# The end of a fused attention and expert kernel: last blocks with tokens on partitions, and three smaller edits

## The chip, the cores and the metric

The kernel runs on one core of a Trainium2 chip. A core has a matrix engine (TensorE, PE in the profile; its weight loads are shown apart as PEld), three engines for elementwise work (VectorE or DVE, ScalarE or ACT, GpSimd or POOL) and queues that issue transfers (SP, and ACT's and POOL's own). They run side by side, each in its own order, and wait for one another on semaphores. Matrix products go to PSUM, in banks of 512 float32 per partition; PE, DVE and ACT work on PSUM, POOL here only on SBUF. The metric is the device time of one execution in microseconds: 448.48 us, the median of three runs (448.10 to 449.16).

## The reference, cut to what matters

A polynomial attention is followed by four experts, all of which every token goes through:

```python
q_p, k_p = phi(q), phi(k)                  # 64 products of two 8-wide sketches
num = q_p @ (k_p.T @ v);  den = q_p @ k_p.sum(0) + 1e-06
x = (num / den)                            # (4, 4, 1088, 32) -> 4352 tokens x 128
p = domain_probs / (domain_probs.sum(-1, keepdims=True) + 1e-09)
for e in range(4):                         # w1: 128 x 1024, w2: 1024 x 128
    h = np.maximum(x @ w1[e], 0.0)
    out += p[:, e:e + 1] * (h @ w2[e])
```

Everything is float32.

## The kernel before

The experts take nearly all the time. Tokens are cut into ten chunks (`CHUNKS`, line 105): 128, 448, six of 480, two of 448. Activations lie transposed, with features on partitions and tokens along the columns. A step `i` of the main loop is a chunk `m`, an expert `e` and a pair of the eight 128-wide blocks of the hidden layer; its two halves, one block each, are the half-steps that plans and due times count. There are 160 steps; `work()` counts half-steps in `now` and runs whatever `lay_plan` has put down for that count: the attention of later tokens, which is spread between the expert's work by hand (`UNITS_AT`: for each unit of queries the half-steps of its transpose, of its two products, and of its use).

First layer, per block (`first`, `third`): three matmuls in a fast float32 form with operands split in a high and two low parts, `xa·wa` (L1140), `xb·wb` (L1141), ACT scales the sum in PSUM (L1142), and one half-step later `xd·wd` (L1192). A block then goes one of two ways. A three-part block: ACT writes the high part `ha` (L1196), DVE the low part `hb` (L1168) and, for two blocks at once, `hd` (L1171), and the second layer multiplies three parts. A plain block: ACT writes the relu (L1201) and the second layer multiplies it in full float32, four times the columns' time, in two records on PE.

Second layer: `to_due` puts each product on a list with its half-step by the `DEAL` tables (a letter for the part, x for plain; a number for the block), and `behind` issues what is due. Products a and b go to one PSUM bank (o0), d and x to the other (o1); `last_of` names the one that ends a bank. When o0 ends, ACT scales it to SBUF (`ev`, L1268). When o1 ends, `gather` adds it to ev, POOL multiplies by the gate row (L1337) and adds to `total` (L1339). For chunks before the seventh the addition of o1 is done by DVE (L1324); from the seventh on ACT copies o1 (L1327) and POOL adds (L1330). `ev` has one buffer.

The last chunk's last expert (`at_end`) has six three-part blocks (0, 1, 3, 4, 5, 6) and then two plain ones (2, 7), and an ending of its own: POOL gates and adds o0's share in two halves (L1272, L1273), while the last matmul is cut in two halves; then per half DVE multiplies o1 by the gate (L1288), adds the total (L1289), transposes 32x32 squares (L1290), and four stores write runs of 32 floats (L1293), on SP's and ACT's queues.

The query units: a unit's projection goes to memory (`qd`) and comes back with rows repeated in `qp` and `qb` (L779, L781); `unit_product` multiplies the two on DVE (L793). Each chunk's tokens are split in parts four and three steps before its first (L893 on ACT, L896 on DVE). The key projection (L458) multiplies 128-wide weights by 128 columns in plain float32.

Of the kernel before, what the change touches and what calls it, by code (L numbers as in the profile page):

```python
# [7 lines left out]

F32 = mybir.dt.float32
BF16 = mybir.dt.bfloat16  # L10
# [2 lines left out]
ALU = mybir.AluOpType  # L13
# [11 lines left out]
def kernel(  # L25
# [24 lines left out]
    nc = tc.nc  # L50

    P = 128
# [33 lines left out]
        b5=9, a6=9, a7=9, b6=10, b7=10, d4=10, d5=11, d6=11, d7=12,  # L86
    )
    DEAL_END = dict(
        a0=4, b0=4, a1=4, b1=5, a2=5, a3=5, d0=6, d1=6, b2=6, a4=7, b3=7, a5=8, b4=8, d2=8, d3=8,
        b5=9, d4=10, d5=10, x6=10, x7=11,  # L90
    )
    ALL_IN = {(7, 2), (8, 2), (9, 2)}
    UNITS = [[P, 448, 512], [576, 512], [576, 512], [576, 512]]
# [7 lines left out]
    W2_AT = (36, 37, 38, 39, 40), (40, 41, 42, 43, 44), (45, 46, 48, 50, 53), (51, 53, 56, 60, 63)  # L101
    TOKENS_AT = 11, 12

    CHUNKS = [P, 448] + [480] * 6 + [448] * 2
    NC = len(CHUNKS)
    MORE_IN = {(2, 2), (3, 2), (4, 2), (5, 0), (5, 2), (5, 3), (6, 2), (7, 0), (7, 1), (7, 2), (7, 3), (8, 0), (8, 1), (8, 2), (8, 3), (9, 0), (9, 1), (9, 2)}
    MORE_AT = {0: (73, 75), 1: (56, 57), 2: (38, 39), 3: (77, 78)}
# [85 lines left out]

    def last_of(m, e, o):
        deal = deal_of(m, e)
        return max((p for p in deal if (p[0] in "ab") == (o == 0)), key=lambda p: (deal[p], list(deal).index(p)))

    def split_at(b):
        return (THREE if in_three(b) else OTHER).index(b)
# [175 lines left out]
    def parts(m):  # L375

        c, end, at = START[m], START[m] + CHUNKS[m], 0
        while c < end:
            n = min(end, (c // S + 1) * S) - c
            yield c // S, c % S, n, at  # L380
            c, at = c + n, at + n
# [420 lines left out]
    def add(hs, run):  # L802
# [9 lines left out]

    UNITS_AT = (
        (30, 43, 44, 47), (41, 71, 77, 79), (68, 103, 106, 111), (102, 134, 137, 143), (132, 161, 171, 175),
        (172, 180, 196, 207), (200, 217, 219, 223),
    )

    def lay_plan():
# [253 lines left out]
    def at_end(m, e):  # L1072
        return (m, e) == (NC - 1, E - 1)
# [85 lines left out]
    def hidden():  # L1159
        return mpool.tile([P, CW], F32, tag="hid", bufs=4, name="hid")  # L1160
# [26 lines left out]
    def third():  # L1187

        while begun:
            i, j, k, g, w, x = begun.pop(0)  # L1190
            n = g.shape[-1]
            nc.tensor.matmul(g, w, x, start=False, stop=True, skip_group_check=True)  # L1192
            m, e = steps[i][0], steps[i][1] // NP
            if k in three_of(m, e) and not whole(m, e):
                (ha, hb, hc), both_of = three_tiles(k, n, three_of(m, e))
                nc.scalar.activation(ha, g, ACTF.Relu, scale=NEAR)  # L1196
                to_lower.append((g, ha.bitcast(F32), hb, both_of))
                hid[i][j] = ha, hb, hc
            else:
                hid[i][j] = hidden()[:, 0:n]  # L1200
                nc.scalar.activation(hid[i][j], g, ACTF.Relu)  # L1201

    def second(i, j=None):

# [47 lines left out]
    def passed(m, e, what, k, hd):  # L1252

        n, o = CHUNKS[m], 0 if what in "ab" else 1
        if (m, e) not in acc:
            acc[m, e] = [None, None]
        if acc[m, e][o] is None:
            acc[m, e][o] = psum(ps_o, f"o{o}")
        first_one = (m, e, o) not in begun_o
        begun_o.add((m, e, o))  # L1260
        last = last_of(m, e, o) == what + str(k)
        b = block_of(m, e, k)
        w, h = (second_weight(e, b), hd) if what == "x" else (w2_parts[e][b]["abd".index(what)], hd["abd".index(what)])
        for x in halves(n) if last and o and at_end(m, e) else [slice(0, n)]:
            nc.tensor.matmul(acc[m, e][o][:, x], w, h[:, x], start=first_one, stop=last, skip_group_check=at_end(m, e))  # L1265
        if last and o == 0:
            evs[m, e] = mpool.tile([P, CW], F32, tag="ev", bufs=1, name="ev")
            nc.scalar.activation(evs[m, e][:, 0:n], acc[m, e][0][:, 0:n], ACTF.Copy, scale=1.0 + R12)  # L1268
            if at_end(m, e):
                ev, g = evs.pop((m, e)), gate[m, e]  # L1270
                for x in halves(n):
                    nc.gpsimd.tensor_tensor(out=ev[:, x], in0=ev[:, x], in1=g[:, x], op=ALU.mult)  # L1272
                    nc.gpsimd.tensor_tensor(out=total[m][:, x], in0=total[m][:, x], in1=ev[:, x], op=ALU.add)  # L1273
        if last and o == 1:
            finish(m, e) if at_end(m, e) else close(m, e)

    def halves(n):
        return slice(0, n // 64 * 32), slice(n // 64 * 32, n)

    def finish(m, e):  # L1280

        n = CHUNKS[m]
        ((b, c, _, _),) = parts(m)
        o1, g, whole_sum = acc.pop((m, e))[1], gate.pop((m, e)), total.pop(m)
        rest = mpool.tile([P, CW], F32, tag="rest", bufs=1, name="rest")
        ob = mpool.tile([P, CW], F32, tag="ob", bufs=1, name="ob")
        for x in halves(n):
            nc.vector.tensor_tensor(out=rest[:, x], in0=g[:, x], in1=o1[:, x], op=ALU.mult)  # L1288
            nc.vector.tensor_tensor(out=rest[:, x], in0=rest[:, x], in1=whole_sum[:, x], op=ALU.add)  # L1289
            nc.vector.transpose(ob[:, x], rest[:, x])  # L1290
            t, r = (c + x.start) // 32, (x.stop - x.start) // 32
            for a in range(4):
                (nc.scalar if a % 2 else nc.sync).dma_start(  # L1293
                    bass.AP(out.tensor, out.offset + (b * S + t) * DM + 32 * a, [[G * DM, 32], [DM, r], [1, 32]]),
                    _ap(ob, 32 * a, 32, x.start, [[32, r], [1, 32]]),
                )

    def turn_back(m, src):

# [14 lines left out]
    def gather(m, e):  # L1314

        n = CHUNKS[m]
        o0, o1 = acc.pop((m, e))
        if o0 is None:
            ev = mpool.tile([P, CW], F32, tag="ev", bufs=1, name="ev")
            nc.vector.tensor_copy(ev[:, 0:n], o1[:, 0:n])  # L1320
        else:
            ev = evs.pop((m, e))
            if m < 7 and (m, e) not in FAR_ADD:
                nc.vector.tensor_tensor(out=ev[:, 0:n], in0=ev[:, 0:n], in1=o1[:, 0:n], op=ALU.add)  # L1324
            else:
                rest = mpool.tile([P, CW], F32, tag="rest", bufs=1, name="rest")
                nc.scalar.copy(rest[:, 0:n], o1[:, 0:n])  # L1327
                for c in range(0, n, 256):
                    x = slice(c, min(c + 256, n))
                    nc.gpsimd.tensor_tensor(out=ev[:, x], in0=ev[:, x], in1=rest[:, x], op=ALU.add)  # L1330
        g = gate.pop((m, e))[:, 0:n]
        if e == 0:
            total[m] = mpool.tile([P, CW], F32, tag="total", bufs=1, name="total")
        for c in range(0, n, 256):
            x = slice(c, min(c + 256, n))
            to = total[m] if e == 0 else ev
            nc.gpsimd.tensor_tensor(out=to[:, x], in0=ev[:, x], in1=g[:, x], op=ALU.mult)  # L1337
            if e:
                nc.gpsimd.tensor_tensor(out=total[m][:, x], in0=total[m][:, x], in1=ev[:, x], op=ALU.add)  # L1339
        yield  # L1340
        later = m + (e + 2) // E
        if later < NC:
            load_gates(later, [(e + 2) % E])
        if e == E - 1:
            yield
            yield
            turn_back(m, total.pop(m)[:, 0:n])
# [81 lines left out]
    for i in range(len(steps) + LA):  # L1429
        if i == len(steps):  # L1430
            behind(2 * i)
            third()
            lower()
        if i < len(steps):
            m, kq = steps[i]
            assert have[0] >= START[m] + CHUNKS[m]

            def work():

                now[0] += 1  # L1440
                for part in at_half.get(now[0] - 1, ()):
                    part()
                for run in plan.pop(now[0], ()):
                    run()

            first(i, work, lambda j: behind(2 * i + j))
            to_due(i)
            if kq == NQ - 4 and 0 < m < NC - 1:
                assert have[0] >= START[m + 1] + CHUNKS[m + 1]
            for part in to_part.get(i, ()):  # L1450
                part()
            if i == 2:
                gate_quotients()
            elif i == 8:
                later_weights()
            elif i == 5:
                load_batch(1)
            elif i == 24:
                load_batch(2)
            elif i == 12:  # L1460
                gate_rows()
            elif i == 13:
                later_mask()
                store_gates(range(1))
            elif i in (18, 20):
                load_gates(1, [(i - 18) // 2], nc.gpsimd)
            elif 14 <= i < 14 + B - 1:
                store_gates(range(i - 13, i - 12))
        if i == LA:

            made_hp[3] = psum(ps_h, "h")
            for c in (0, HP):
                half_columns(3, made_hp[3], c)
        if not behind(2 * i + 1):
            next(ending, None)
# [30 lines left out]
```

## Time and profile before

| | |
|---|---|
| median of the runs | 448.48 us (448.10 to 449.16) |
| the profiled execution | 448.93 us, span 446.9 us |
| TensorE granted clock, mean | 0.994 |
| PE, DVE, ACT, POOL busy | 97%, 86%, 77%, 38% |
| PE idle in 246 to 300 us | 0.92 us |
| last matmul ends, last store issued | 438.8, 443.4 us |

The profile is of one execution. A line of a timeline has the start and the duration in us, the engine, the kernel's line and the operation with its tiles; "x6" merges six instructions, and brackets hold the idle time before it and who ended it. Matmul records overlap: a record lasts longer than the step to the next one, and steps from start to start tell PE's pace. A line by stretch has, after the limits, its length, then busy time and number of instructions of PE, PEld, DVE, ACT and POOL, the granted clock, the share of the transfer engines and GB/s. In the list of waits a line has who waited, for whom, the total, the number of times and the longest. SPq and ACTq lines are transfers being issued.

### The profile page before, as it was taken

What the parts mean: (1) busy time and instruction counts of PE and PEld (TensorE: products, weight loads), DVE (VectorE), ACT (ScalarE), POOL (GpSimd) and SP (SyncE); (2) the same over time, 40 slices, a digit from 0 to 9 for tenths busy, and PEclk for the clock granted to TensorE, in tenths of its full rate; (3) what the DMA queues carried; (4) which work ended last, traced back from release to release, by engine and by line L of the source; (5) the groups of instructions that cost most, each with busy time, mean ns of one, the idle gap of its engine ahead of it and who ended that gap; (6) DMA issues with size and microseconds to landing.
All of it is one profiled execution on the core that took longest, in us unless ns stands there. A gap on an engine that the chain in (4) does not pass through costs nothing.

```text
span 446.9 us, 8094 instructions
## 1 busy us (share of the span) xinstructions
PE 435.2 (97%) x2752; PEld 357.7 (80%) x2752; DVE 385.4 (86%) x612; ACT 345.9 (77%) x722; POOL 168.3 (38%) x246
## 2 busy tenths in 40 slices
PE   8999999999999999999999999999999999999992
PEld 5787678888887888778887778787888888888891
DVE  5898969978999889989997798889988998898893
ACT  4478888758878688868884797677788988898881
POOL 6349623212142023213351245133334463456454
PEclk9999999999999999999999999999999999999997
DMA  8955366224502330234114601251320012002001
GB/s 222 279 141 162 86 162 126 78 50 127 149 23 45 113 99 23 73 83 142 23 28 69 154 9 43 47 146 37 69 45 22 23 34 52 22 21 42 22 21 21
DMA packets 46873, 35.01 MB, mean 78 GB/s; under 512 B 23472, under 2 KB 41616, under 8 KB 46832
## 3 DMA queue, kind: packets, MB, share of 16 engines
q1 hardware_dynamic: 44528, 33.26, 30.0%
q0 software_dynamic: 1184, 1.05, 0.9%
q8 instruction: 21, 0.34, 0.3%
q10 hardware_dynamic: 1120, 0.19, 0.3%
q14 instruction: 20, 0.16, 0.1%
HBM read 29.27 MB, written 5.21 MB: 77 GB/s over the span
## 4 chain that ended last, share of the span: by engine, by line
PE 89%; DMA 4%; POOL 2%; DVE 1%; SPq 1%; ACT 1%; issue 1%; POOLq 0%; DVEq 0%; ACTq 0%
PE o L1265 39%; PE h L1140 13%; PE h L1141 13%; PE h L1192 13%; PE h L271 6%; PE o L1245 3%; DMA w_sb<-in_moe_w_dram 2%; PE h L458 1%; DMA qb<-qd 1%; PE o L271 1%; DMA dp<-in_moe_domain_probs_dram 1%; SPq L177 1%; POOL total L1339 0%; ACT h L1142 0%; DMA s_raw<-in_S_dram 0%
## 5 line engine op out<-in xcount | busy, mean ns | idle before, releaser
L1142 ACT ACTIVATE h<-h 128x480 f32<-128x480 f32 (+1 forms) x288 | 158.8, 552 | 63.4 <-PE h L1141 58.3
L1168 DVE SCALAR_TENSOR_TENSOR hb<-h,ha 128x480 fp32r<-128x480 f32 (+1 forms) x225 | 140.6, 639 | 27.6 <-ACT ha L1196 25.8
L1171 DVE SCALAR_TENSOR_TENSOR hd<-ha,hb 128x960 fp32r<-128x960 f32 (+3 forms) x120 | 137.8, 1149 | 11.7 <-DVE hb L1168 0.5
L1140 PE MATMUL h<-xa,wa 128*128 128x480 f32 (+1 forms) x288 | 129.4, 449 | 0.0
L1196 ACT ACTIVATE ha<-h 128x480 fp32r<-128x480 f32 (+1 forms) x225 | 126.2, 561 | 1.7 <-PE h L1192 1.6
L1192 PE MATMUL h<-xd,wd 128*128 128x480 f32 (+1 forms) x288 | 108.7, 377 | 0.1
L1141 PE MATMUL h<-xb,wb 128*128 128x480 f32 (+1 forms) x288 | 108.0, 375 | 0.0
L1337 POOL TENSOR_TENSOR ev<-ev,gate 128x256 f32<-128x256 f32 (+2 forms) x52 | 45.6, 878 | 141.6 <-DVE ev L1324 133.6
L1265 PE MATMUL o<-ha,vab 128*128 128x480 f32 (+1 forms) x204 | 76.8, 377 | 0.0
L1140 PEld LDWEIGHTS h<-xa,wa 128*128 128x128 f32 x288 | 54.2, 188 | 17.8 <-issue 11.3
L1141 PEld LDWEIGHTS h<-xb,wb 128*128 128x128 f32 x288 | 54.2, 188 | 17.5 <-issue 11.7
L1265 PE MATMUL o<-hd,vd 128*128 128x480 f32 (+1 forms) x204 | 63.7, 379 | 0.0
L1192 PEld LDWEIGHTS h<-xd,wd 128*128 128x128 f32 x288 | 54.0, 188 | 8.9 <-ACT h L1142 1.0
L1339 POOL TENSOR_TENSOR total<-total,ev 128x256 f32<-128x256 f32 (+2 forms) x52 | 55.1, 1060 | 4.1
L1265 PE MATMUL o<-hb,vb 128*128 128x480 f32 (+1 forms) x136 | 51.4, 378 | 0.9 <-DVE hb L1168 0.9
L1330 POOL TENSOR_TENSOR ev<-ev,rest 128x256 f32<-128x256 f32 (+2 forms) x26 | 19.0, 752 | 70.8 <-ACT rest L1327 70.8
L1265 PE MATMUL o<-hid,w_sb 128*128 128x480 f32 (+2 forms) x96 | 44.8, 551 | 0.0
L1265 PEld LDWEIGHTS o<-hd,vd 128*128 128x128 f32 x204 | 37.8, 188 | 6.0 <-issue 0.8
L1265 PEld LDWEIGHTS o<-ha,vab 128*128 128x128 f32 x204 | 38.3, 188 | 5.1
L1201 ACT ACTIVATE hid<-h 128x480 f32<-128x480 f32 (+1 forms) x63 | 35.3, 560 | 1.5 <-PE h L1192 1.4
L1337 POOL TENSOR_TENSOR total<-ev,gate 128x256 f32<-128x256 f32 (+2 forms) x18 | 15.7, 896 | 38.4 <-issue 23.0
L1265 PEld LDWEIGHTS o<-hb,vb 128*128 128x128 f32 x136 | 25.5, 188 | 5.8 <-DVE hb L1168 2.1
(157 smaller groups left out, 460.9 us busy)
## 6 DMA issues: line engine op xcount, KB each, us to landing
gate<-gates SPq DMA_DIRECT2D x14, 224.0 KB
gate<-gates SPq DMA_DIRECT2D x12, 240.0 KB, 3.4
kn<-in_k_dram SPq DMA_DIRECT2D x4, 544.0 KB
vn<-in_v_dram SPq DMA_DIRECT2D x16, 128.0 KB, 5.5
qp<-qd SPq DMA_DIRECT2D x8, 256.0 KB
qp<-qd SPq DMA_DIRECT2D x6, 288.0 KB, 5.1
qb<-qd SPq DMA_DIRECT2D x6, 288.0 KB
qn<-in_q_dram SPq DMA_DIRECT2D x3, 544.0 KB
```

The costliest lines, as they stand in the source:

```text
L271: nc.tensor.matmul(out(s), weights(s), moving(s), **flags)
L1140: nc.tensor.matmul(g, wa[:, e, w], xa, start=True, stop=False)
L1141: nc.tensor.matmul(g, wb[:, e, w], xb, start=False, stop=True)
L1142: nc.scalar.activation(g, g, ACTF.Copy, scale=1.0 + R12)
L1168: nc.vector.scalar_tensor_tensor(out=hb, in0=g, scalar=0.0, in1=high, op0=ALU.max, op1=ALU.subtract)
L1171: nc.vector.scalar_tensor_tensor(out=d2, in0=a2.bitcast(F32), scalar=R12, in1=b2.bitcast(F32), op0=ALU.mult, op1=ALU.subtract)
L1192: nc.tensor.matmul(g, w, x, start=False, stop=True, skip_group_check=True)
L1196: nc.scalar.activation(ha, g, ACTF.Relu, scale=NEAR)
L1201: nc.scalar.activation(hid[i][j], g, ACTF.Relu)
L1265: nc.tensor.matmul(acc[m, e][o][:, x], w, h[:, x], start=first_one, stop=last, skip_group_check=at_end(m, e))
L1337: nc.gpsimd.tensor_tensor(out=to[:, x], in0=ev[:, x], in1=g[:, x], op=ALU.mult)
L1339: nc.gpsimd.tensor_tensor(out=total[m][:, x], in0=total[m][:, x], in1=ev[:, x], op=ALU.add)
```

## The change

Four edits. The last chunks become 480 and 416 columns wide. The first product of query unit 5 moves from half-step 180 to 186. The sum of the last chunk's expert 2 is done by DVE. And the last expert's end is done otherwise: its two plain blocks are gated behind the relu (one by DVE in one step, the other by ACT and then POOL), and multiplied as the stationary operand, so that the result has tokens on partitions in a bank of its own; the six three-part blocks are gated and added to the total by DVE in two slices, and brought into the same bank by a product with an identity. Three copies and four stores of whole rows of 128 floats end the kernel.

```diff
     DEAL_END = dict(
-        a0=4, b0=4, a1=4, b1=5, a2=5, a3=5, d0=6, d1=6, b2=6, a4=7, b3=7, a5=8, b4=8, d2=8, d3=8,
-        b5=9, d4=10, d5=10, x6=10, x7=11,
+        a0=4, b0=4, a1=4, b1=5, a2=5, a3=5, d0=6, d1=6, b2=6, a4=7, b3=7, a5=8, b4=8, d2=9, d3=9,
+        b5=9, d4=10, d5=10, x6=11, x7=11,
     )
-    CHUNKS = [P, 448] + [480] * 6 + [448] * 2
+    CHUNKS = [P, 448] + [480] * 7 + [416]
     def last_of(m, e, o):
-        return max((p for p in deal if (p[0] in "ab") == (o == 0)), key=...)
+        return max((p for p in deal if p[0] in ("ab" if o == 0 else "d" if at_end(m, e) else "dx")), key=...)
     UNITS_AT = (
-        (172, 180, 196, 207), (200, 217, 219, 223),
+        (172, 186, 196, 207), (200, 217, 219, 223),
     # third()
                 hid[i][j] = hidden()[:, 0:n]
+                if at_end(m, e) and k == N3:
+                    nc.vector.scalar_tensor_tensor(
+                        out=hid[i][j], in0=g, scalar=0.0, in1=gate[m, e][:, 0:n], op0=ALU.max, op1=ALU.mult
+                    )
+                    continue
                 nc.scalar.activation(hid[i][j], g, ACTF.Relu)
+                if at_end(m, e):
+                    nc.gpsimd.tensor_tensor(out=hid[i][j], in0=hid[i][j], in1=gate[m, e][:, 0:n], op=ALU.mult)
     # passed()
+        if what == "x" and at_end(m, e):
+            return by_token(m, e, k, hd)
...
-        for x in halves(n) if last and o and at_end(m, e) else [slice(0, n)]:
-            nc.tensor.matmul(acc[m, e][o][:, x], w, h[:, x], start=first_one, stop=last, ...)
+        nc.tensor.matmul(acc[m, e][o][:, 0:n], w, h, start=first_one, stop=last)
...
-            if at_end(m, e):
-                ev, g = evs.pop((m, e)), gate[m, e]
-                for x in halves(n):
-                    nc.gpsimd.tensor_tensor(out=ev[:, x], in0=ev[:, x], in1=g[:, x], op=ALU.mult)
-                    nc.gpsimd.tensor_tensor(out=total[m][:, x], in0=total[m][:, x], in1=ev[:, x], op=ALU.add)
     def finish(m, e):
-        (per half: gate times o1, plus total, transpose on DVE; four stores of 32-float runs)
+        n, o1, ev, g = CHUNKS[m], acc.pop((m, e))[1], evs.pop((m, e)), gate.pop((m, e))
+        for x in (slice(0, 2 * P), slice(2 * P, n)):
+            nc.vector.tensor_tensor(out=ev[:, x], in0=ev[:, x], in1=o1[:, x], op=ALU.add)
+            nc.vector.tensor_tensor(out=ev[:, x], in0=ev[:, x], in1=g[:, x], op=ALU.mult)
+            nc.vector.tensor_tensor(out=ev[:, x], in0=ev[:, x], in1=total[m][:, x], op=ALU.add)
+        last_sum[0] = ev
+    def by_token(m, e, k, hd):
+        n = CHUNKS[m]
+        if last_rows[0] is None:
+            last_rows[0] = psum(ps_h, "h")
+            last_rows.append(lpool.tile([P, 4 * P], F32, tag="kn", name="rows"))
+        y, rows = last_rows
+        cols = [(c, min(P, n - c)) for c in range(0, n, P)]
+        for c, w in cols:
+            nc.tensor.matmul(y[0:w, c : c + P], hd[:, c : c + w], second_weight(e, block_of(m, e, k)),
+                start=(k == N3 and c == 0), stop=False, skip_group_check=True)
+        if k < FB - 1:
+            return
+        for c, w in cols:
+            nc.tensor.matmul(y[0:w, c : c + P], last_sum[0][:, c : c + w], eye[0][:, :],
+                start=False, stop=True, skip_group_check=True)
+        ((b, at, _, _),) = parts(m)
+        nc.scalar.copy(rows[:, 0 : 2 * P], y[:, 0 : 2 * P])
+        nc.vector.tensor_copy(rows[:, 2 * P : 3 * P], y[:, 2 * P : 3 * P])
+        nc.vector.tensor_copy(rows[0 : n - 3 * P, 3 * P :], y[0 : n - 3 * P, 3 * P :])
+        for queue, c in ((nc.sync, 0), (nc.scalar, 2), (nc.sync, 1), (nc.scalar, 3)):
+            c, w = cols[c]
+            queue.dma_start(bass.AP(out.tensor, out.offset + (b * S + (at + c) // 32) * DM,
+                [[DM, w // 32], [G * DM, 32], [1, DM]]), rows[0:w, c : c + P])
+    def later_eye():                       # called after step NQ * (NC - 2), chunk 8's first
+        eye[0] = apool.tile([P, P], F32, tag="qb", name="eye")
+        make_identity(nc, eye[0][:, :])    # a memset and a selection on POOL
     # gather()
-            if m < 7 and (m, e) not in FAR_ADD:
+            if (m < 7 and (m, e) not in FAR_ADD) or (m, e) == (NC - 1, E - 2):
                 nc.vector.tensor_tensor(out=ev[:, 0:n], in0=ev[:, 0:n], in1=o1[:, 0:n], op=ALU.add)
```

More of the change, by code (lines that the diff above doesn't have):

```diff
@@ L7 @@
 from concourse._compat import with_exitstack
+from concourse.masks import make_identity
 F32 = mybir.dt.float32
@@ L195, in last_of @@
         deal = deal_of(m, e)
-        return max((p for p in deal if (p[0] in "ab") == (o == 0)), key=lambda p: (deal[p], list(deal).index(p)))
+        return max((p for p in deal if p[0] in ("ab" if o == 0 else "d" if at_end(m, e) else "dx")), key=lambda p: (deal[p], list(deal).index(p)))
     def split_at(b):
@@ L1263, in passed @@
         w, h = (second_weight(e, b), hd) if what == "x" else (w2_parts[e][b]["abd".index(what)], hd["abd".index(what)])
-        for x in halves(n) if last and o and at_end(m, e) else [slice(0, n)]:
-            nc.tensor.matmul(acc[m, e][o][:, x], w, h[:, x], start=first_one, stop=last, skip_group_check=at_end(m, e))
+        nc.tensor.matmul(acc[m, e][o][:, 0:n], w, h, start=first_one, stop=last)
         if last and o == 0:
@@ L1268, in passed @@
             nc.scalar.activation(evs[m, e][:, 0:n], acc[m, e][0][:, 0:n], ACTF.Copy, scale=1.0 + R12)
-            if at_end(m, e):
-                ev, g = evs.pop((m, e)), gate[m, e]
-                for x in halves(n):
-                    nc.gpsimd.tensor_tensor(out=ev[:, x], in0=ev[:, x], in1=g[:, x], op=ALU.mult)
-                    nc.gpsimd.tensor_tensor(out=total[m][:, x], in0=total[m][:, x], in1=ev[:, x], op=ALU.add)
         if last and o == 1:
             finish(m, e) if at_end(m, e) else close(m, e)
-    def halves(n):
-        return slice(0, n // 64 * 32), slice(n // 64 * 32, n)
@@ L1280, in finish @@
     def finish(m, e):
-        n = CHUNKS[m]
[L1283 to L1296, printed above, removed]
+        n, o1, ev, g = CHUNKS[m], acc.pop((m, e))[1], evs.pop((m, e)), gate.pop((m, e))
@@ new lines, in finish @@
+        for x in (slice(0, 2 * P), slice(2 * P, n)):
[3 more added lines that the diff above has]
+        last_sum[0] = ev
+    last_sum, last_rows = [None], [None]
+    def by_token(m, e, k, hd):
+        n = CHUNKS[m]
+        if last_rows[0] is None:
[4 more added lines that the diff above has]
+        for c, w in cols:
+            nc.tensor.matmul(
+                y[0:w, c : c + P], hd[:, c : c + w], second_weight(e, block_of(m, e, k)),
+                start=(k == N3 and c == 0), stop=False, skip_group_check=True,
+            )
+        if k < FB - 1:
+            return
+        for c, w in cols:
+            nc.tensor.matmul(
+                y[0:w, c : c + P], last_sum[0][:, c : c + w], eye[0][:, :],
+                start=False, stop=True, skip_group_check=True,
+            )
+        ((b, at, _, _),) = parts(m)
[4 more added lines that the diff above has]
+            c, w = cols[c]
+            queue.dma_start(
+                bass.AP(out.tensor, out.offset + (b * S + (at + c) // 32) * DM, [[DM, w // 32], [G * DM, 32], [1, DM]]),
+                rows[0:w, c : c + P],
+            )
@@ L1298, in turn_back @@
+    eye = [None]
+    def later_eye():
+        eye[0] = apool.tile([P, P], F32, tag="qb", name="eye")
+        make_identity(nc, eye[0][:, :])
     def turn_back(m, src):
@@ L1461 @@
                 gate_rows()
+            elif i == NQ * (NC - 2):
+                later_eye()
             elif i == 13:
```

## The prediction

> **What bounds the kernel now.** I read the page first, then busy time by stretch, then the waits and the order of time around the two places where the chain leaves the matrix engine.
>
> ```profile
> span 446.9 us, 8094 instructions
> PE 435.2 (97%) x2752; PEld 357.7 (80%) x2752; DVE 385.4 (86%) x612; ACT 345.9 (77%) x722; POOL 168.3 (38%) x246
> ```
>
> By stretch (us, then PE busy) the matrix engine (PE) has no gap between 104 and 431 us but one, and then the end, where it works for half of the time:
>
> ```profile
> 246.00:300.00 54.00, 53.08 (x268) 42.38 (x267) 45.32 (x64) 41.95 (x84) 16.44 (x19) 1.00 0.33 77
> 343.00:388.00 45.00, 45.00 (x213) 39.54 (x212) 40.68 (x55) 39.16 (x81) 25.05 (x26) 1.00 0.13 29
> 431.00:447.00 16.00, 7.82 (x37) 6.40 (x35) 8.07 (x13) 5.53 (x12) 8.22 (x10) 0.83 0.10 15
> ```
>
> So whatever does not lengthen PE's stream or open a gap is hidden until 431. The gap, from the waits (first line) and the order of time:
>
> ```profile
> DVE qp L793 <- DMA qb<-qd: 2.0, 1, 2.0
> ...
> 254.06 1.07 DVE L793 TENSOR_TENSOR qp<-qp,qb 128x576 f32<-128x576 f32 x1 [1.99 <-DMA qb<-qd]
> 254.22 0.38 PE L1140 MATMUL h<-xa,wa 128*128 128x480 f32 x1
> 255.06 0.64 DVE L1168 SCALAR_TENSOR_TENSOR hb<-h,ha 128x480 fp32r<-128x480 f32 x1
> 255.76 0.49 PE L1265 MATMUL o<-hb,vb 128*128 128x480 f32 x1 [0.51 <-DVE hb L1168]
> 256.09 0.38 PE L1140 MATMUL h<-xa,wa 128*128 128x480 f32 x1
> 257.52 0.49 PE L1265 MATMUL o<-hb,vb 128*128 128x480 f32 x1 [0.41 <-DVE hb L1168]
> 258.28 0.38 PE L1140 MATMUL h<-xa,wa 128*128 128x480 f32 x1
> ```
>
> VectorE (DVE) is held 1.99 us by a query transfer issued at 248.05, and the low parts (hb) behind it come late to PE. Start to start of L1140 gives the loss: the half-step from 254.22 has five matmuls and lasts 1.87, a like one (268.85 to 269.95) 1.10; the next has seven and lasts 2.19, a like one (267.33 to 268.85) 1.52. That is 0.77+0.67 = 1.44 us, and no later gap absorbs it.
>
> The end, in order of time:
>
> ```profile
> 436.63 0.30 PEld L1265 LDWEIGHTS o<-hd,vd 128*128 128x128 f32 x2 [0.27 <-DVE hd L1171]
> 437.15 1.67 PE L1265 MATMUL o<-hid,w_sb 128*128 128x448 f32 x6
> 438.43 0.54 ACT L1268 ACTIVATE ev<-o 128x448 f32<-128x448 f32 x1 [1.31 <-POOL total L1339]
> 440.48 0.83 DVE L1289 TENSOR_TENSOR rest<-rest,total 128x224 f32<-128x224 f32 x1 [1.18 <-POOL total L1273]
> 441.78 2.02 SPq L1293 DMA_DIRECT2D out_dram<-ob  x4
> 441.78 2.08 ACTq L1293 DMA_DIRECT2D out_dram<-ob  x4
> 442.13 0.39 DVE L1289 TENSOR_TENSOR rest<-rest,total 128x224 f32<-128x224 f32 x1
> 442.55 0.41 DVE L1290 STREAM_TRANSPOSE ob<-rest 128x224 f32<-128x224 f32 x1
> ```
>
> GpSimd (POOL) still adds expert 2 when PE is done: ScalarE (ACT) gets ev only at 438.43, POOL scales and adds both halves after that, DVE follows half by half, and eight stores leave, the last at 443.4 (by the view of that line). The span ends 3.5 us after.
>
> **The change, part by part.**
>
> *Product moved from half-step 180 to 186.* It issues no transfer, only one DVE operation, 0.67 to 0.84 us without a wait. Its data landed at 254.04; the new place is near 260, so the wait goes: 1.44 us. Queued behind it there are the token part xb (L896, 0.65) and hb of block 1, which PE reads at 264.29, 2.0 us after it was done. The hb of block 4 is the tightest: done near 267.5, read at 268.20. But in the trace hb of block 0 starts 0.58 after its ha (259.39+0.57 to 260.54), a lag left by the stall that goes with it, so 0.7 later becomes 0.1 to 0.3 and fits. Bounds: gain 1.44, or as low as 0.4 if the lag meets contention (L1171 took 1.57 us at 265.39 where 1.16 is usual). I take 1.4, since the slack rows cover the median.
>
> *Chunk widths 480 and 416 for 448 and 448.* A matmul step is 0.2175 us at 480 and 0.2035 at 448, so 0.014 for 32 columns. Chunk 8 has 195 such steps (3 experts of 24+21+4, one of 48), chunk 9 without its last plain blocks 188: +2.73-2.63 = +0.1. It ends with narrower work, which I count below. Token, gate and store transfers change size with the chunk and stay far ahead: 0.
>
> *Identity.* Two POOL operations at chunk 8's start (340 to 350 us), where POOL is partly free. The trace has no such selection; nearest are a 128x768 memset, 0.74, and a 128x256 product, 0.74 to 1.6. Below nothing is excluded, as it only adds work. POOL's gathers behind it have microseconds of room, and one late DVE operation costs at most its excess of 0.4: 0, at most 0.4.
>
> *Expert 2's sum on DVE.* ACT's copy (0.54) and POOL's two adds (2.15 together) go; DVE gains one sum from PSUM, 0.61 at 448 columns, 0.58 at 416. Queued behind it are hb of block 3, then both hd pairs, for which PE waits. All positions below are on this profile's clock, ahead of the 1.44. DVE's last pair ended at 436.58. Add 0.58, and 0.55 because the remaining 32 matmuls, narrower, start later against the same end (32x0.014, and the 0.1); take off 0.26 for narrower operations, and 0 to 0.4 for the pair that ran 1.49 instead of 1.09 beside POOL's adds: 437.05 to 437.45, I take 437.2. PE, ready at 436.6, waits 0.6 where it waited 0.27. The parts d2 and d3, moved behind the last first-layer matmul, only fill PE earlier: 0; their pair is done by 435.2.
>
> *The end itself.* d4, d5 by 437.65, readable 437.8. The gated relu of block 6 is a DVE step like L1168, 0.58: 437.2 to 437.8. Block 7's gate goes to POOL: POOL has four operations of expert 2 from 433.2, 2.4 us free or up to 4.0 contended, so 435.7 to 437.2, then a 416-wide product, 1.2 by L1272's 0.66 for 224 or 2.4 contended: 437.9 to 439.6. The token-major matmuls are full float32, 128 moving columns, new weights each time. The same form is in the key projection:
>
> ```profile
> 104.39 1.06 PE L458 MATMUL h<-sk,kT 128*128 128x128 f32 x8
> 105.20 0.47 PE L1265 MATMUL o<-ha,vab 128*128 128x480 f32 x1
> ```
>
> Eight records in 0.89 (by the chain), 0.111 each. Two blocks of eight records and eight of joining: block 6 from 437.8 to 438.7, block 7 to 439.6 (2.7 us of PE in all, where the old blocks took 1.67). DVE sums meanwhile from 437.8: 256 columns in three steps of 0.43 (L468's 0.416 for 256 from PSUM) to 439.2, 160 columns to 440.2. So the joins run 439.6 to 440.5, readable 440.75. L1288 started its first half only when PE's second was over, so I let all copies wait for the last join: ACT 0.37 (L766's 256), DVE 0.28 twice (L689's 128): 441.35. Two issues per queue instead of four, 0.42 each: the last starts at 441.65, against 443.4. A 64 KB transfer lands in 1.9 (xd<-y) where these landed in 1.7. So -1.75+0.2 = -1.55; as its unknowns lean to later, I take -1.5. Bounds: -1.9 (pair at 437.05, no contention) to -0.1 (pair 0.25 later, POOL 0.9 later, the reads of the one bank taking turns 0.3).
>
> *A rule against it.* L1289 took 0.83 at 440.48, beside a POOL product, and 0.39 alone at 442.13: 0.44 more. The Trainium skill, page "SBUF — State Buffer", section "Who interferes with whom", says that a DVE instruction with two SBUF inputs contends with a GpSimd instruction that reads SBUF, and that the one which comes second is blocked for the whole instruction. By that rule the gate product of block 7 could hold the sums or be held by them, and the sum would be the fourth rival's; the L1289 rows agree with it in direction.
>
> *Sum.* -1.4+0.1-1.5 = -2.8. The profiled execution took 448.93 (span 446.9 and 2.0 around it): 446.1. It lies 0.45 above the median of 448.48, so for the median 445.7.
>
> **The rivals.**
> 1. Only the stall goes, and the end keeps its length since joins and copies cost what POOL's chain did: 448.48-1.3 = 447.2. For it: PE's work at the end grows by 1.0. Against: POOL's four operations (2.8 us from 439.05 to 441.82) leave the chain.
> 2. The end shortens, but at the new place xb and the product together delay hb and PE waits there instead: 448.48-1.5+0.2, 447.2. For it: DVE is without idle time from 254 to 270.6. Against: over 1 us between hb and its reader in most half-steps.
> 3. Slower: the token-major matmuls cannot hide their weights. 24 records at 0.188 (a load) plus 0.111 are 7.2 us for 2.7, +4.5: 450.2. It decides from 0.111+2.8/24 = 0.23 us a record. Against: the L458 rows are the same form with new weights each time.
> 4. The port: the gate product meets the last hd pair and DVE's sums, 0.44 for each of two meetings: 446.6.
> 5. The gap only moves and the end is no shorter: 448.5, no change.
>
> **How the numbers follow.** Forecast 0.50 (445.0 to 446.4 by its own bounds), port 0.12, stall only 0.13, end only 0.11, no change 0.05, slower 0.09. Faster by over 0.2% (0.9 us, about what this kernel's spread of 448.1 to 449.16 lets one tell) is the first four, 0.86; lowered to 0.84 for rivals that end near 447.6. Same 0.06, slower 0.10. The range has to take in 447.2 with its spread: 444.7 to 447.7.
>
> **What would show it.** After: no wait of L793 for a transfer and no gap of PE near 255; DVE's sum in place of ACT's copy; ACT's ev no longer after POOL by more than 0.2; the token-major records 0.11 apart; the joins starting when DVE's second slice is done; the last store issued some 3 us earlier than 443.4. The prediction is wrong if PE has a new gap near 260, if the records are 0.2 apart or more, or if the joins wait beyond 441 for POOL's product.

## The result, and the profile after

The changed kernel takes 447.24 us (median of 22 runs, 446.97 to 448.23) against 448.08 us before (22 runs, 447.25 to 449.16): a ratio of 0.9985, 95% interval 0.9978 to 0.9991. It is faster by 0.8 us, where 2.8 were forecast, and less than the 0.2% that the prediction took as its bound. The direction was right, the size was not. The time itself lies inside the stated range of 444.7 to 447.7, but that is partly luck: the forecast started from 448.48, and these runs of the kernel before have a median of 448.08.

The span of the profiled execution went from 446.9 to 445.1 us, which is more than the medians moved. The first L1140 matmul of the new execution (L1141 in its numbering) starts at 28.1 us where the old one started at 29.1, so about 1.0 of the 1.8 us comes from the start, which the change does not touch. The other 0.8 agrees with the medians.

The page's head, and by stretch the time around the old gap and the end:

```profile
span 445.1 us, 8123 instructions
PE 437.4 (98%) x2770; PEld 359.6 (81%) x2770; DVE 386.5 (87%) x616; ACT 345.4 (78%) x721; POOL 166.7 (37%) x243
246.00:300.00 54.00, 54.00 (x275) 43.88 (x274) 46.76 (x66) 43.00 (x86) 19.42 (x20) 1.00 0.34 81
431.00:447.00 16.00, 7.75 (x45) 6.14 (x44) 6.71 (x14) 3.41 (x8) 4.97 (x5) 0.87 0.06 15
```

PE is busy for all of 54.00 us where it was for 53.08. DVE around the product's new place shows why:

```profile
256.20 0.66 DVE L1172 SCALAR_TENSOR_TENSOR hd<-ha,hb 128x480 fp32r<-128x480 f32 x1
257.49 0.66 DVE L1169 SCALAR_TENSOR_TENSOR hb<-h,ha 128x480 fp32r<-128x480 f32 x1 [0.63 <-PE h L1142]
258.07 0.75 DVE L794 TENSOR_TENSOR qp<-qp,qb 128x576 f32<-128x576 f32 x1
258.73 0.65 DVE L897 SCALAR_TENSOR_TENSOR xb<-xa,ring 128x480 fp32r<-128x480 f32 x1
```

Its product (L794) waits for nothing, and DVE even has 0.63 us of idle time before the step ahead of it (L1169), which fits a lag of the stall that is gone.

The end, in order of time:

```profile
433.69 1.03 DVE L1172 SCALAR_TENSOR_TENSOR hd<-ha,hb 128x832 fp32r<-128x832 f32 x1
433.75 1.35 POOL L1370 TENSOR_TENSOR total<-total,ev 128x160 f32<-128x160 f32 x1
434.77 0.30 PEld L1274 LDWEIGHTS o<-hd,vd 128*128 128x128 f32 x2 [0.54 <-DVE hd L1172]
435.06 1.06 POOL L1209 TENSOR_TENSOR hid<-hid,gate 128x416 f32<-128x416 f32 x1
435.13 0.52 ACT L1277 ACTIVATE ev<-o 128x416 f32<-128x416 f32 x1 [0.57 <-POOL total L1370]
435.27 2.47 PE L1301 MATMUL h<-w_sb,hid 128*128 128x128 f32 x16
437.65 0.32 DVE L1287 TENSOR_TENSOR ev<-ev,total 128x160 f32<-128x160 f32 x1
437.67 1.27 PE L1308 MATMUL h<-eye,ev 128*128 128x128 f32 x8
438.98 0.37 ACT L1313 COPY rows<-h 128x256 f32<-128x256 f32 x1 [3.33 <-PE h L1308]
439.38 1.25 SPq L1318 DMA_DIRECT2D out_dram<-rows  x2
439.39 0.29 DVE L1314 COPY rows<-h 128x128 f32<-128x128 f32 x1 [1.42 <-ACT rows L1313]
439.71 1.22 ACTq L1318 DMA_DIRECT2D out_dram<-rows  x2
```

From the first of the last two hd matmuls to the end of the span it is 446.9-436.63 = 10.3 us before and 445.1-434.77 = 10.3 after. The old chain of POOL and DVE is gone, and the end is as long as it was. The last store is issued at 440.5, 2.9 us earlier than before, but the span ends only 1.8 earlier. Of both, 1.0 is the earlier start and about 1.4 the stall that is gone, so what else was changed brings the last issue forward by some 0.5 us and puts the end of the span back by some 0.6. The transfers of this stretch, from 438.5 to 445.1 us (share of the 16 engines in tenths, 40 slices; then the issues):

```profile
DMA  0000000040000122322222243522220000000000
...
DMA packets 445, 0.23 MB, mean 35 GB/s; under 512 B 28, under 2 KB 444, under 8 KB 444
...
out_dram<-rows SPq DMA_DIRECT2D x2, 64.0 KB
out_dram<-rows ACTq DMA_DIRECT2D x1, 64.0 KB
out_dram<-rows ACTq DMA_DIRECT2D x1, 16.0 KB, 3.5
```

and the same view of the kernel before, from 441 to 447 us:

```profile
DMA  0000000000078868821796697100000000000010
...
out_dram<-ob SPq DMA_DIRECT2D x4, 28.0 KB, 1.7
```

A store of the old end landed 1.7 us after its issue, with the transfer engines 0.6 to 0.9 busy but for a dip between the two halves. The last one of the new end lands after 3.5, and through most of its 2.9 us of data the engines are 0.2 busy, where four of sixteen would be 0.25.

### The profile page after: what moved, and what is told of

The parts are those of the page before. It is cut to its first block, busy times and chain, and to the rows that moved or that the text cites. A ratio compares the mean times of both kernels' runs of the same rounds, so it can differ in the third digit from the quotient of the medians.

```text
span 445.1 us, 8123 instructions
## 1 busy us (share of the span) xinstructions
PE 437.4 (98%) x2770; PEld 359.6 (81%) x2770; DVE 386.5 (87%) x616; ACT 345.4 (78%) x721; POOL 166.7 (37%) x243
## 4 chain that ended last, share of the span: by engine, by line
PE 92%; DMA 3%; DVE 1%; SPq 1%; ACT 1%; issue 1%; POOL 0%; DVEq 0%; ACTq 0%
PE o L1274 40%; PE h L1141 14%; PE h L1142 14%; PE h L1193 14%; PE h L272 6%; PE o L1253 3%; DMA w_sb<-in_moe_w_dram 2%; PE h L459 1%; PE o L272 1%; DMA dp<-in_moe_domain_probs_dram 1%; PE h L1301 1%; DVE hb L1169 0%; ACT h L1143 0%; SPq L178 0%; DMA s_raw<-in_S_dram 0%
## 5 line engine op out<-in xcount | busy, mean ns | idle before, releaser
L1143 ACT ACTIVATE h<-h 128x480 f32<-128x480 f32 (+2 forms) x288 | 158.9, 552 | 63.8 <-PE h L1142 56.5
L1169 DVE SCALAR_TENSOR_TENSOR hb<-h,ha 128x480 fp32r<-128x480 f32 (+2 forms) x225 | 140.5, 639 | 28.2 <-ACT ha L1197 25.8
L1172 DVE SCALAR_TENSOR_TENSOR hd<-ha,hb 128x960 fp32r<-128x960 f32 (+4 forms) x120 | 137.9, 1149 | 11.6 <-DVE hb L1169 0.5
L1141 PE MATMUL h<-xa,wa 128*128 128x480 f32 (+2 forms) x288 | 129.5, 450 | 0.0
L1197 ACT ACTIVATE ha<-h 128x480 fp32r<-128x480 f32 (+2 forms) x225 | 126.3, 561 | 0.1
L1193 PE MATMUL h<-xd,wd 128*128 128x480 f32 (+2 forms) x288 | 108.7, 377 | 0.1
L1142 PE MATMUL h<-xb,wb 128*128 128x480 f32 (+2 forms) x288 | 108.0, 375 | 0.0
L1274 PE MATMUL o<-ha,vab 128*128 128x480 f32 (+2 forms) x204 | 76.7, 377 | 0.0
L1141 PEld LDWEIGHTS h<-xa,wa 128*128 128x128 f32 x288 | 54.2, 188 | 18.0 <-issue 11.4
L1274 PE MATMUL o<-hd,vd 128*128 128x480 f32 (+2 forms) x204 | 63.7, 379 | 0.2 <-DVE hd L1172 0.2
L1370 POOL TENSOR_TENSOR total<-total,ev 128x256 f32<-128x256 f32 (+3 forms) x52 | 55.7, 1072 | 4.1
```

Source lines behind the costliest of these rows:

```text
L1141: nc.tensor.matmul(g, wa[:, e, w], xa, start=True, stop=False)
L1142: nc.tensor.matmul(g, wb[:, e, w], xb, start=False, stop=True)
L1143: nc.scalar.activation(g, g, ACTF.Copy, scale=1.0 + R12)
L1169: nc.vector.scalar_tensor_tensor(out=hb, in0=g, scalar=0.0, in1=high, op0=ALU.max, op1=ALU.subtract)
L1172: nc.vector.scalar_tensor_tensor(out=d2, in0=a2.bitcast(F32), scalar=R12, in1=b2.bitcast(F32), op0=ALU.mult, op1=ALU.subtract)
L1274: nc.tensor.matmul(acc[m, e][o][:, 0:n], w, h, start=first_one, stop=last)
```

## The experiments

Two theories had to be told apart for each half. For the gain: the move is worth the whole stall, and the rest costs 0.6 (A), or the move is worth just the 0.8 and the rest is neutral (B). For the end: the new stores are slow by the shape in which they are written (C), or for their row size or their place (D). Other letters are explained in the expectations that use them. All times below are medians, against runs of the kernel before on the same chip (448.16 to 448.25); the changed kernel's are the 447.24 and the gain of 0.8 from above. A ratio with its interval is a summary of the same runs by itself: it can differ from the quotient of the medians by up to 0.0009, or 0.4 us, so gains less than half a microsecond apart are not told apart.

**The move alone**, on the kernel before:

```diff
-        (172, 180, 196, 207), (200, 217, 219, 223),
+        (172, 186, 196, 207), (200, 217, 219, 223),
```

> The kernel before, with only the product of query unit 5 moved from half-step 180 to 186. Theory A (the move is worth its whole stall, and the rest of the change costs about 0.6 us): 1.4 us faster than before, no gap of PE near 255 us. Rival B (the stall of the profiled execution was longer than usual; the move explains just the measured gain and the rest is neutral): about 0.8 us faster.

446.83 against 448.16, ratio 0.9977 (0.9966 to 0.9987): 1.3 us faster (1.0 by the ratio), and PE is busy for all of its 246 to 300 us.

**The change without the move**, the same line put back in the changed kernel:

```diff
-        (172, 186, 196, 207), (200, 217, 219, 223),
+        (172, 180, 196, 207), (200, 217, 219, 223),
```

> The changed kernel with the product back at half-step 180, so widths, sum, gating and new end without the move. Theory A: about 0.6 us slower than before. Rival B: equal to before within 0.2 us.

448.80 against 448.16, ratio 1.0019 (1.0010 to 1.0029): 0.6 us slower. From its waits and its order of time:

```profile
DVE qp L794 <- DMA qb<-qd: 1.7, 1, 1.7
...
253.26 0.76 DVE L794 TENSOR_TENSOR qp<-qp,qb 128x576 f32<-128x576 f32 x1 [1.70 <-DMA qb<-qd]
```

The stall is back, with 1.70 us of waiting. Both runs say A: the move is worth 1.3 to 1.5 us, and the widths, the sum and the new end together cost 0.6. The interval of this run excludes B's no change; that of the move alone, 0.6 to 1.5 us, still holds B's 0.8 and does not exclude it by itself.

**The move and the widths, with the old end:**

```diff
-    CHUNKS = [P, 448] + [480] * 6 + [448] * 2
+    CHUNKS = [P, 448] + [480] * 7 + [416]
```

> The kernel before with the move and the widths 480 and 416, but the old end. Theory A with the step of 0.014 us for 32 columns: 1.3 us faster than before, so the widths by themselves cost 0.1. If narrower work at the end shortens the old chain of POOL and DVE instead (416 for 448 in some eight operations of it, 0.03 each), 1.5 us faster.

446.58, ratio 0.9972 (0.9964 to 0.9981). It cannot be told from the move alone (0.9977), so the widths neither cost nor bring what these runs can show. And it is 0.7 us below the changed kernel. The two intervals just overlap, but the run before says the same: the new end and what feeds it are what costs.

**The stores with their outer dimensions exchanged:**

```diff
-                bass.AP(out.tensor, ..., [[DM, w // 32], [G * DM, 32], [1, DM]]),
+                bass.AP(out.tensor, ..., [[G * DM, 32], [DM, w // 32], [1, DM]]),
```

> The changed kernel with the two outer dimensions of the last stores' target exchanged (32 rows of the stride G*DM outermost, then the group of tokens), in the same four stores of the same bytes; it leaves the order of the rows wrong, so the last 416 tokens land on one another's rows. Theory C (a store is spread over no more transfer engines than its outermost dimension has entries, four here, so 64 KB takes 1.0 us on its own and the next queues behind it): the last data lands about 1.0 to 1.4 us earlier than in the changed kernel, and the kernel is 1.8 to 2.2 us faster than before. Rival D (the 512-byte rows or the late issue are slow in themselves): no earlier landing, 0.8 us faster than before as the changed kernel is.

445.92, ratio 0.9959 (0.9945 to 0.9972): 2.2 us faster than before, 1.3 faster than the changed kernel. The number of stores, their bytes and their 512-byte runs are the same. From 437 to 444 us:

```profile
DMA  0000000000000000000000047388700000000000
...
DMA packets 480, 0.21 MB, mean 30 GB/s; under 512 B 64, under 2 KB 480, under 8 KB 480
...
out_dram<-rows ACTq DMA_DIRECT2D x1, 16.0 KB, 1.7
```

The engines are 0.7 to 0.8 busy in most of the slices with data, and the last store lands after 1.7 us instead of 3.5. This is C. The last store, of 16 KB, has a single group of 32 rows, so it is the same transfer in both kernels: what delayed it were the three stores of 64 KB before it. The small packets fit this. Beside 416 rows of 512 bytes there are 28 packets under 512 bytes in the changed kernel and 64 here, and 32 in a run below with eight entries outermost: 3x4+16, 4x16 and 4x8. That is one for each engine used, if a store goes to as many engines, up to 16, as its outermost dimension of more than one entry has entries. The Trainium skill, page "DMA: Bandwidth & Descriptors", section "Why a DMA increments its semaphore by 16 and not by 1", says that a transfer is spread over the largest number of engines up to 16 that divides the slowest dimension of more than one entry in both of its access patterns. With four groups of tokens outermost that is four engines, and with 32 rows 16; the 0.2 and the 0.8 busy and the small packets agree with it, and the prediction did not weigh it.

**Four groups of 128 tokens**, the last one overlapping:

```diff
+        wide = [(c, min(c, n - P)) for c, _ in cols]
-        for c, w in cols:
-            nc.tensor.matmul(y[0:w, c : c + P], hd[:, c : c + w], ...)
+        for c, a in wide:
+            nc.tensor.matmul(y[:, c : c + P], hd[:, a : a + P], ...)
```

(and the same for the joins; the stores take the last 32 rows of the fourth group)

> The changed kernel, but the fourth group of tokens is taken 128 wide too (columns 288 to 416, so 96 tokens are computed twice and only the last 32 rows are stored). Theory E (a weight load of another width than the one before is not pulled ahead, which puts gaps of 0.09 to 0.1 us around each 32-wide group and makes 24 records last 3.7 us instead of 2.7): 8 records in 0.9 instead of 1.2 us; the joins then wait for the second slice of DVE, so the last join ends 0.4 us earlier and the kernel is 1.2 us faster than before (0.8 as the changed kernel is). Rival F (the gaps stand at every new group of matmuls, whatever its width): no difference to the changed kernel.

447.15 against 448.19, ratio 0.9976 (0.9966 to 0.9986), which cannot be told from the changed kernel. Its order of time:

```profile
435.53 2.08 PE L1302 MATMUL h<-w_sb,hid 128*128 128x128 f32 x16
437.45 0.67 PE L1309 MATMUL h<-eye,ev 128*128 128x128 f32 x4
437.91 0.33 DVE L1287 TENSOR_TENSOR ev<-ev,total 128x160 f32<-128x160 f32 x1
438.29 0.71 PE L1309 MATMUL h<-eye,ev 128*128 128x128 f32 x4 [0.17 <-DVE ev L1287]
```

Two things follow. The 32-wide group was what made the records slow: sixteen take 2.08 us where they took 2.47, with more columns loaded. And it was worth nearly nothing, because the joins, counted from the start of the last hd matmuls, end only about 0.2 us earlier: the second half of them now waits for DVE's second slice. PE's records and DVE's sums end together; a shorter one alone hardly shortens the end.

**Two PSUM banks:**

```diff
-            last_rows[0] = psum(ps_h, "h")
+            last_rows[0] = [psum(ps_h, "h"), psum(ps_h, "h")]
-        nc.scalar.copy(rows[:, 0 : 2 * P], y[:, 0 : 2 * P])
-        nc.vector.tensor_copy(rows[:, 2 * P : 3 * P], y[:, 2 * P : 3 * P])
+        nc.scalar.copy(rows[:, 0 : 2 * P], y[0][:, 0 : 2 * P])
+        nc.vector.tensor_copy(rows[:, 2 * P : 3 * P], y[1][:, 0:P])
```

> The changed kernel with its result in two PSUM banks, so that ACT and DVE can copy at the same time. DVE's copies should start 0.4 us earlier and the stores of ACT's queue be issued 0.3 earlier. Theory C (the three stores of 64 KB share the same four transfer engines and pass one after the other, 1.0 us each, from the first one on): nothing gained at the end, 0.8 faster than before as the changed kernel is. Rival G (the end is set by the last issue): 1.1 us faster than before.

446.82, ratio 0.9970 (0.9960 to 0.9981): 1.4 us faster than before, some 0.5 better than the changed kernel (the two intervals just overlap), where theory C was made to say nothing.

```profile
437.73 1.27 PE L1308 MATMUL h<-eye,ev 128*128 128x128 f32 x8
438.48 0.37 ACT L1313 COPY rows<-h 128x256 f32<-128x256 f32 x1 [2.77 <-PE h L1308]
438.88 1.25 SPq L1318 DMA_DIRECT2D out_dram<-rows  x2
439.04 0.29 DVE L1314 COPY rows<-h 128x128 f32<-128x128 f32 x1 [1.01 <-PE h L1308]
```

That expectation overlooked ACT's copy: with a bank of its own it no longer waits for the other two joins, and starts 438.48-437.73 = 0.75 us after the joins do, where it was 1.31. So the first store leaves 0.5 us earlier, and a row of transfers that pass one after the other ends earlier by what its first gains. The run does not separate C from G.

**Equal groups of 104 tokens**, columns laid by rows (8 rows of 13 tokens), two banks, stores with 8 entries outermost:

```diff
-                        out=hid[i][j], in0=g, scalar=0.0, in1=gate[m, e][:, 0:n], ...
+                        out=in_rows(hid[i][j]), in0=by_place(g), scalar=0.0, in1=by_place(gate[m, e][:, 0:n]), ...
+    # by_place: "p (t s) -> p s t", in_rows: "p (s t) -> p s t"; the same in ACT's, POOL's and DVE's other steps
-    [[DM, w // 32], [G * DM, 32], [1, DM]]
+    [[G * DM, 8], [DM, 13], [1, DM]]
```

> All three together, with the right result: columns are laid so that four equal groups of 104 tokens hold 8 rows of 13 tokens each, two PSUM banks, two copies, and stores whose outermost dimension has 8 entries. If the causes add up (stores 1.3, weight widths 0.4, bank 0.3 against the changed kernel's 0.8): 2.8 us faster than before. If strided reads or writes of 13 by 32 slow DVE, ACT or POOL: DVE steps of the end longer than 0.42 for 208 columns, and 2.0 us.

446.50, ratio 0.9962 (0.9948 to 0.9975): 1.7 us, less than the 2.0 of the worse case. The layout costs a good part of what the stores give back:

```profile
434.73 0.89 DVE L1203 SCALAR_TENSOR_TENSOR hid<-h,gate 128x416 f32<-128x416 f32 x1
436.34 0.53 DVE L1300 TENSOR_TENSOR rest<-rest,gate 128x208 f32<-128x208 f32 x1
439.07 0.69 PE L1323 MATMUL h<-eye,rest 128*104 128x128 f32 x4 [0.84 <-DVE rest L1301]
```

The gated relu reads with a stride and takes 0.89 us for 0.58; a sum of 208 columns takes 0.53, more than the 0.42 of 256 columns in order; and PE waits 0.84 for the second slice. An issue of these stores also lasts longer, 0.68 to 0.80 us.

**Expert 2's sum on ACT and POOL as before:**

```diff
-            if (m < 7 and (m, e) not in FAR_ADD) or (m, e) == (NC - 1, E - 2):
+            if m < 7 and (m, e) not in FAR_ADD:
```

> The changed kernel with expert 2's last sum back on ACT and POOL. The wait of PE for the last hd pair should fall from 0.7 to 0.2 or 0.3 us, and POOL's chain end some 1.5 us later, so that ev and with it DVE's sums come later. Theory H (POOL's chain would set the end again): 0.3 us slower than before to 0.2 faster, thus 0.6 to 1.1 slower than the changed kernel. Rival I (DVE's added sum delays PE and costs more than it saves): 1.2 us faster than before.

449.02, ratio 1.0017 (1.0008 to 1.0026): 0.8 us slower than before, 1.7 slower than the changed kernel, beyond what H expected.

```profile
434.85 0.30 PEld L1274 LDWEIGHTS o<-hd,vd 128*128 128x128 f32 x2 [0.34 <-DVE hd L1172]
435.95 0.52 POOL L1370 TENSOR_TENSOR total<-total,ev 128x160 f32<-128x160 f32 x1
436.43 1.06 POOL L1209 TENSOR_TENSOR hid<-hid,gate 128x416 f32<-128x416 f32 x1
436.50 0.52 ACT L1277 ACTIVATE ev<-o 128x416 f32<-128x416 f32 x1 [1.66 <-POOL total L1370]
437.54 1.27 PE L1301 MATMUL h<-w_sb,hid 128*128 128x128 f32 x8 [0.92 <-POOL hid L1209]
```

POOL's gate product is queued behind POOL's adds, so PE waits 0.92 us for block 7, besides the later ev. The wait for the last hd pair did shrink, from 0.54 to 0.34 us by the row of the weight load, but not to what was expected in full, as the pair step before it took 1.39 us beside POOL's adds where it took 1.17. The sum on DVE is a necessary part of the new end.

**The right rows, the stores cut by partitions:**

```diff
-        for queue, c in ((nc.sync, 0), (nc.scalar, 2), (nc.sync, 1), (nc.scalar, 3)):
-            c, w = cols[c]
-            [[DM, w // 32], [G * DM, 32], [1, DM]]   <-  rows[0:w, c : c + P]
+        for queue, t in ((nc.sync, 0), (nc.scalar, 1), (nc.sync, 2), (nc.scalar, 3)):
+            r = n // P + (t < n % P // 32)
+            [[G * DM, 32], [4 * DM, r], [1, DM]]     <-  _ap(rows, 32 * t, 32, 0, [[P, r], [1, P]])
```

> The changed kernel with right rows and four stores cut another way: each takes 32 partitions and all four column groups, so that its outermost dimension has 32 entries; nothing else is changed. Every store now waits for the last copy, 0.5 us later than the first one did. Theory C (spread over 16 engines, the data takes well under 1 us): the last data lands about 1.1 us earlier than in the changed kernel, 1.8 to 2.2 us faster than before. Rival D (it was the wrong order of rows that made the earlier trial fast): 0.8 as the changed kernel, or less.

445.90 against 448.25, ratio 0.9951 (0.9938 to 0.9963): 2.3 us faster than before. From 437 to 444 us:

```profile
DMA  0000000000000000000000067899600000000010
...
out_dram<-rows SPq DMA_DIRECT2D x1, 48.0 KB, 1.7
```

Only the cut of the four stores differs from the changed kernel (one of 64 KB and three of 48, all issued behind the last copy), and it gains what the exchanged dimensions gained. D falls: rows, runs and place are the same.

**All that helped**, with groups that start at columns 0, 96, 192 and 288, two banks, one copy on each engine, and slices of 224 and 192:

```diff
+        at_col = [96 * i for i in range(4)]
+        to = lambda i: y[i // 2][:, P * (i % 2) : P * (i % 2) + P]
+        nc.scalar.copy(rows[:, 0 : 2 * P], y[0][:, 0 : 2 * P])
+        nc.vector.tensor_copy(rows[:, 2 * P :], y[1][:, 0 : 2 * P])
+        for queue, t, a, r in ((nc.sync, 0, 0, 4), (nc.scalar, 1, 0, 4), (nc.sync, 2, 0, 4), (nc.scalar, 3, 3, 1)):
+            [[G * DM, 32], [3 * DM, r], [1, DM]]     <-  _ap(rows, 32 * t, 32, P * a, [[P, r], [1, P]])
```

> Those stores, with the result in two PSUM banks and four groups of 128 tokens that overlap (starts 0, 96, 192, 288), DVE's slices 224 and 192 wide. Against the stores alone: 0.3 to 0.5 for the copies that run side by side, 0.2 for the load gaps, so 2.4 to 2.8 us faster than before. If DVE's sums are what ends last before the joins, not the records: 2.2 to 2.4.

445.90, ratio 0.9945 (0.9931 to 0.9958), the fastest ratio of all, though five runs don't tell it from the stores alone (0.9951). The gain is 2.3 us by the medians, within the expectation's second case. PE waits for DVE's second slice here too, so the sums, and not the records, hold the last joins:

```profile
438.31 0.71 PE L1309 MATMUL h<-eye,ev 128*128 128x128 f32 x4 [0.24 <-DVE ev L1287]
```

## Why the prediction was wrong

**The move: right.** It was put at 1.4 us from the starts of L1140; alone it measured 1.3. The second rival, that product and token part together would delay hb, fell: no gap, and no lag to add to.

**The widths: right within what can be told.** 0.1 was said, and the run shows no difference.

**Identity: right as far as shown.** It was given no cost, and nothing in the chain of the end waits for it; no run takes it out.

**Expert 2's sum, hd pair, gates: about right.** PE was to wait 0.6 us for the last pair where it waited 0.27 by the row of the weight load; by the same row it waited 0.54. ACT's ev was to be free of POOL by 0.2, and still waits 0.57 for it. POOL's gate product took 1.06, not up to 2.4, and nothing waits for it.

The rule on the shared port, and the rival made of it, were about that product. It was over at 436.12, before DVE's next step with two SBUF inputs began at 436.14, so the two did not meet. But the contention shows one step earlier. POOL's last add of expert 2 (L1370, 160 columns) began at 433.75, 0.06 us behind DVE's pair step, which reads ha and hb from SBUF, and took 1.35 us; with no DVE step beside it, in the run with the sum on ACT and POOL, the same add took 0.52. That agrees with the rule. POOL's four operations of expert 2 so took 4.0 us, the prediction's upper bound, and ACT's ev had to wait for the last of them. What this costs no run shows: the joins of the changed kernel do not wait for the sums behind ev, while those of the last run wait 0.24 us for them.

**The end itself: the step that failed.** It was to bring 1.5 us, and the changed kernel is 0.7 slower than the same kernel with the old end. The terms, as the prediction put them:

| term | said | measured in the changed kernel |
|---|---|---|
| token-major records and joins, from the first to readable | 437.8 to 440.75, 2.95 us | 435.27 to 438.94, 3.67 us |
| copies after that | 0.6 | 0.9, DVE waits for ACT |
| last issue after the copies | 0.3 | 0.6, an issue lasts 0.60 instead of 0.42 |
| landing of the last store | 1.9, against 1.7 before | 3.5, against 1.7 |

The four terms were 2.9 us too small together. Of this 2.2 is the miss: the 1.5 that was to be gained and the 0.7 that was lost. The rest came back: the first record stood 0.50 behind the pair's start where 0.6 was said, and the span ended 1.1 us after the last landing where it had ended 1.8 after by 443.4+1.7.

The last term is most of it: 1.6 us too little by the profile, and 1.3 to 1.5 by the two runs that changed only the stores. It was taken from a row with as many bytes (xd<-y, 64 KB, 1.9), but that transfer has 32 entries in its outermost dimension, and three of the new stores have four; the last store has to wait behind them. The row was near in bytes and far in shape. With the stores mended, the kernel takes 445.9 us, about 0.7 less than with the old end and the same widths (446.58). So even then the new end brings half of the 1.5; the remaining 0.8 lies in the other terms.

The records: 0.111 us holds inside a run of 128-wide groups, as in the key projection, but not around the 32-wide one, where each block loses 0.2 us. The prediction's sign of slow records, 0.2 us apart or more, so came true at the changes of width only. The run with full groups shows that the 32-wide group is the cause; it counts little, because DVE's sums end at the same time. That the copies might take turns stood in the prediction as an upper bound of 0.3 and came out as 0.3.

The first rival, that only the stall goes and the end keeps its length, is nearest to what happened. It was given 0.13 and 447.2 us. That the measured 447.24 lies on it is in part luck, as its gain was 1.3 us and the measured one 0.8. Its reason, that joins and copies cost what POOL's chain did, holds in part, since they took 1.0 us longer than said; the stores, which are most of the miss, it did not name. One sign of the forecast also came true in part by luck: the last store is issued 2.9 us earlier, of which 1.0 is the earlier start.

What stays open: after the last data the span goes on for about 1.6 us in the changed kernel and 2.0 before. No run looked for the cause, and it is in none of the terms.

## What to carry to other kernels

Before a store's time is taken from another row, compare the outermost dimension of both sides and not only the bytes: the same 208 KB in four stores cost 1.3 to 1.5 us more at the end of the kernel when four entries stood outermost in three of them. At an end where nothing hides a transfer, look at the busy share of the transfer engines, since 0.2 for microseconds was the trace of stores on four of sixteen. And where PE's records and DVE's sums end together, a shorter one alone brings next to nothing, so move the step that both wait for, or what comes after them.

## What the runs showed of the hardware that was not expected

- A weight load of another width than the one before it opens a gap in the float32 stream: sixteen records with 128 and 32 wide groups took 2.47 us, sixteen of 128 wide 2.08, and sixteen of 104 wide 1.99.
- A DVE read with a stride of 32 elements is dearer than one in order: 0.89 against 0.58 us for the gated relu of 416 columns, 0.53 for 208 against 0.42 for 256 in a sum.
- An issue of a store of 128 partitions with rows of 512 bytes lasted 0.58 to 0.66 us in the changed kernel, one of 32 partitions 0.34 to 0.46 there and in the run cut by partitions, and one of the old stores 0.32 to 0.46.
